# The half block of the first layer follows a table of orders; the product of the small-value gelu becomes a step of its own

## The chip, the cores and the metric

The kernel runs on one core of one Trainium2 chip. The metric is the time of one execution on the device in microseconds (us), the median of several runs. The core's engines each work through a queue of their own in order: TensorE (PE for its matmuls, PEld for its weight loads), VectorE (DVE), ScalarE (ACT), GpSimd (POOL), and SyncE (SP), which only issues DMAs here. They wait for each other through semaphores.

## The reference

```python
# attention with 32 memory rows: batch 8, 8 heads, 576 tokens, head size 64
a = exp(phi - max(phi)); a /= sum(a)                 # over the 32 columns
k_m, v_m = a^T k, a^T v                              # [b, h, 32, 64]
attn = softmax(q k_m^T / 8)                          # [b, h, 576, 32]
x = (attn v_m) with heads side by side               # [4608, 512]
# first layer
h = x @ w_in                                         # [4608, 2048]
x = (h - tanh(h)) @ w_out                            # [4608, 512]
# second layer
h = x @ w_in2
g = where(h > 0, h, exp(min(h, 0)) - 1)
out = g @ w_out2                                     # [4608, 512]
```

The names in the kernel call the function h - tanh(h) of the first layer "g". It is formed in two ways: as a difference where h is large, and as a polynomial product where h is small, since the difference loses digits there. All matmuls of the two layers are done with operands split into a high and a low part, three matmuls for one.

## The kernel before

**Tiling.** The first layer goes through 64 blocks (the loop over `blocks`, L770 to L850). A block is 288 tokens (`n`) by 512 columns of the hidden layer (`sw`), and has two halves (`i`, L809) of 256 hidden columns each. This text counts half blocks from 0 to 127: half 2b is the first half of block b, 2b + 1 its second. The attention units 1 to 15 (generators, `units`), the conversion of the weights from 64-bit words to split 32-bit pairs (generators, `cv`), and the products of the weights with the attention's value rows (`vw_unit`) run between the steps of the half blocks. The second layer follows (L855 to L874).

**A half block.** `h_unit` gives PE 12 matmuls of 288 columns into one of two tiles `h_ps`. On ACT `g_a` forms t = tanh(h), u = h² and s = a square of u; `g_b` forms v = t u on POOL; `g_big` a mask on ACT. On DVE `g_c` forms the difference h - t in place (L394), the product s = (s + G_B) v (L395) and copies the difference over it where the mask is set (L396, `copy_predicated`). The last one frees the `h_ps` tile, which the half after the next one writes. In the next half `g_d` takes the high part of s on ACT (L402) and the low part on POOL (L403). `x_next` gives PE the 12 matmuls of one 128-row piece of x (`x_unit`), of a block about two earlier, into a bank of the pool `ps_m`, and copies them out on ACT (`on_act`, L424) or on DVE (L426). There are two such pieces in a half. `t`, `u`, `v` and the mask have one buffer each, s has two.

**Banks.** The pool `ps_m` has three banks, handed out in turn: to the pieces of x, to the two tiles of a `vw_unit` and to all PSUM tiles of the attention. A tile waits until the bank's former holder has been read.

**Conversions.** One conversion step group costs DVE two instructions (L50 and L51, or L54 and L57) in each half, from block 14 to 57; besides one ACT instruction (L48 or L62), and every second half one on POOL (L64). `cv.round()` moves all conversions by a step, `cv.half()` only those that stand before their first ACT instruction.

**Order.** Nothing reorders: each engine executes in the order in which the program is written (`manual_schedule`), so L811 to L848 set the order on all engines. A `vw_unit` stands ahead of `h_unit` in the second half of each odd block (L811), unless the attention holds it back (`at1.held`); then it comes at L836. `units.round()` is called twice in a half (L832, L846), and lets each live attention unit take one step.

Of the kernel before, what the change touches and what calls it, by code (L numbers as in the profile page):

```python
# [30 lines left out]
G_S = 0.045158483281055074  # L31
G_A = -0.2459677286979875
G_B = 0.27283311065959304


def r32(ap):
# [276 lines left out]
class Moe1:  # L313
# [77 lines left out]
    def g_c(self, n, pg):  # L391
        nc = self.nc
        d, u, t, s, big, v = self.work[n, pg]
        nc.vector.tensor_tensor(d, d, t, op=ALU.subtract)  # L394
        nc.vector.scalar_tensor_tensor(s, s, G_B, v, op0=ALU.add, op1=ALU.mult)  # L395
        nc.vector.copy_predicated(s, big.bitcast(U32), d)  # L396

    def g_d(self, n, pg):
        nc = self.nc
# [143 lines left out]
def moe_kernel(tc, q, k, v, phi, w1, w2, w3, w4, out):  # L543
    nc = tc.nc
    with ExitStack() as top, tc.manual_schedule():
# [157 lines left out]
        def store_late():  # L703
            while late:
                m1.store_x(*late.pop(0))
# [64 lines left out]
        for bi, (ss, bp, sub, j) in enumerate(blocks):  # L770
# [37 lines left out]
            p_there |= p_done  # L808
            for i in range(2):  # L809
                pg = 2 * sw + i  # L810
                if vw_next and bi > 1 and i == 1 and not at1.held:  # L811
                    vw_soon(*vw_next)
                    vw_next = None
                m1.h_unit(sw, n, pg)
                if (bi, i) == (0, 0):
                    cv.round()
                m1.g_a(n, pg)
                m1.g_b(n, pg)
                if i == 1 and bi + 2 < len(blocks):
                    ass, abp, asub, aj = blocks[bi + 2]  # L820
                    far = (2 * ass + asub, 4 * abp + aj)
                    if all(u in p_there for u in range(2 * (far[1] // 2) + 2)):
                        m1.load_p(*far)
                store_late()
                if soon:
                    soon.popleft()()
                x_next(True)
                m1.g_big(n, pg)
                if (bi, i) != (0, 0):
                    cv.round()  # L830
                at1.before_x = True
                units.round()  # L832
                at1.before_x = False
                if pend:
                    m1.g_d(*pend.pop())
                if vw_next and (bi == 1 or i == 1):  # L836
                    vw_soon(*vw_next, i if bi == 1 else None)
                if soon and bi > 60:
                    soon.popleft()()
                x_next(bi < 22)  # L840
                m1.g_c(n, pg)
                cv.half()
                if bi < 7:
                    cv.round()
                    cv.half()
                units.round()  # L846
                pend.append((n, pg))
                next_p(nxt, i == 1)  # L848
            for dm in range(4):
# [55 lines left out]
```

## Time and profile before

| | |
|---|---|
| Median of 3 runs | 1675.61 us (1672.97 to 1678.92) |
| The profiled execution | 1677.41 us, its span 1675.3 us |
| PE busy | 1585.5 us, 95% of the span |
| PEld busy | 1381.5 us, 82% |
| DVE busy | 1201.6 us, 72% |
| ACT busy | 900.9 us, 54% |
| POOL busy | 737.5 us, 44% |

The busy shares are those of the whole span. The first layer's loop ends at about 863 us, and what follows is the second layer, in which PE has almost no gap. A matmul's end is modelled, so that a busy PE can still be waiting between two starts: the pitch from start to start tells how fast it goes. TensorE's granted clock is at its upper level, 2.4 GHz, from about 100 us on, but for a short stretch near 300 us.

### The profile page before, as it was taken

Reading aid. Unit: us, or ns where it says so; the run is one execution under the profiler, and the core shown is the slowest. Engines: PE = TensorE matmul, PEld = TensorE weight load, DVE = VectorE, ACT = ScalarE, POOL = GpSimd, SP = SyncE. Lnnn points to the kernel's source line nnn. Section 1 sums busy time; section 2 is a strip of 40 time slices with the busy share of each in tenths; the row PEclk is TensorE's granted clock in tenths of the full one; section 3 lists DMA queues with packets and bytes.
Section 4 is the critical chain, followed back from the end, with each engine's and each line's share of the span. In section 5 each row is a group of like instructions: output and inputs, shape, how many; then the busy total and the mean of one; then the engine's idle time right before and its main releaser. Section 6 shows DMA issues by size and latency. Waiting matters only on the chain.

```text
span 1675.3 us, 28135 instructions
## 1 busy us (share of the span) xinstructions
PE 1585.5 (95%) x10742; PEld 1381.5 (82%) x10742; DVE 1201.6 (72%) x1680; ACT 900.9 (54%) x1623; POOL 737.5 (44%) x526
## 2 busy tenths in 40 slices
PE   5678989798999999999999999999999999999998
PEld 4557878687999999999999888888888888888886
DVE  5777768878999999999775655656565656555654
ACT  2355768677888888888753333333333333333332
POOL 0245666566775666666642323222232322323222
PEclk9779999999999999999999999999999999999999
DMA  9665667567565456665587321212121212121100
GB/s 238 183 179 159 199 198 238 180 207 240 182 238 170 170 202 214 215 214 189 176 289 279 101 76 38 78 49 76 38 76 46 69 51 63 51 76 51 35 3 26
DMA packets 142214, 232.90 MB, mean 139 GB/s; under 512 B 8704, under 2 KB 102912, under 8 KB 140032
## 3 DMA queue, kind: packets, MB, share of 16 engines
q1 hardware_dynamic: 142080, 231.11, 43.4%
q8 instruction: 84, 1.38, 0.4%
q14 instruction: 50, 0.41, 0.1%
HBM read 157.68 MB, written 73.40 MB: 138 GB/s over the span
## 4 chain that ended last, share of the span: by engine, by line
PE 63%; DVE 9%; issue 2%; POOL 2%; ACT 1%; DMA 0%; DVEq 0%; SPq 0%; POOLq 0%; ACTq 0%
PE h_ps L478 24%; PE o_ps L520 24%; PE x_ps L418 10%; PE h_ps L367 4%; DVE s L395 3%; DVE s L396 2%; DVE h_ps L394 1%; DVE x L426 1%; POOL g L403 1%; POOL v L385 1%; PE vw_ps L349 1%; DVE vw L354 0%; DVE cv_m L50 0%; ACT big L389 0%; DMA p<-p_dram 0%
## 5 line engine op out<-in xcount | busy, mean ns | idle before, releaser
L418 PE MATMUL x_ps<-g,w 128*128 128x288 f32 x3072 | 441.7, 297 | 10.7 <-DVE vw L354 5.4
L504 POOL TENSOR_TENSOR e<-hm,e 128x512 fp32r<-128x512 f32 x144 | 186.7, 1297 | 573.0 <-ACT e L503 529.8
L418 PEld LDWEIGHTS x_ps<-g,w 128*128 128x128 f32 x3072 | 418.0, 189 | 19.0 <-DVE vw L354 9.1
L478 PE MATMUL h_ps<-x,wi 128*128 128x512 f32 (+1 forms) x1920 | 422.2, 370 | 0.0
L520 PE MATMUL o_ps<-wo,e 128*128 128x512 f32 x1728 | 420.3, 392 | 0.7 <-POOL e L504 0.7
L478 PEld LDWEIGHTS h_ps<-x,wi 128*128 128x128 f32 x1920 | 336.0, 188 | 65.7
L520 PEld LDWEIGHTS o_ps<-wo,e 128*128 128x128 f32 x1728 | 323.6, 188 | 72.4 <-POOL e L504 1.1
L489 ACT ACTIVATE t_ps<-hm 128x512 f32<-128x512 f32 x144 | 86.7, 602 | 500.2 <-DVE hm L488 500.2
L385 POOL TENSOR_TENSOR v<-t,u 128x576 f32<-128x576 f32 x128 | 183.5, 1434 | 177.2 <-ACT u L379 129.2
L495 DVE SCALAR_TENSOR_TENSOR hm<-hm,t_ps 128x512 f32<-128x512 f32 x144 | 99.0, 688 | 200.9 <-ACT hm L490 200.9
L367 PE MATMUL h_ps<-p,vw 128*128 128x288 f32 x1536 | 235.5, 303 | 0.0
L403 POOL TENSOR_TENSOR g<-s,g 128x576 fp32r<-128x576 f32 x128 | 192.4, 1503 | 85.8 <-ACT g L402 77.3
L367 PEld LDWEIGHTS h_ps<-p,vw 128*128 128x128 f32 x1536 | 214.1, 192 | 13.7 <-issue 12.4
L395 DVE SCALAR_TENSOR_TENSOR s<-s,v 128x576 f32<-128x576 f32 x128 | 183.7, 1435 | 15.2 <-POOL v L385 15.2
L488 DVE TENSOR_SCALAR hm<-h_ps 128x512 f32<-128x512 f32 x144 | 99.6, 692 | 125.3 <-PE h_ps L478 121.0
L378 ACT ACTIVATE t<-h_ps 128x576 f32<-128x576 f32 x128 | 83.4, 652 | 120.6 <-PE h_ps L367 73.3
L396 DVE COPY_PREDICATED s<-big,h_ps 128x576 f32<-128x576 uint32 x128 | 106.8, 834 | 13.6 <-ACT t L378 0.5
L380 ACT ACTIVATE s<-u,bias 128x576 f32<-128x576 f32 x128 | 99.6, 778 | 20.4 <-POOL g L403 9.8
L394 DVE TENSOR_TENSOR h_ps<-h_ps,t 128x576 f32<-128x576 f32 x128 | 96.9, 757 | 13.4 <-ACT u L379 13.3
L497 DVE TENSOR_TENSOR hm<-hm,h_ps 128x512 f32<-128x512 f32 x144 | 98.9, 687 | 5.0
L496 DVE SCALAR_TENSOR_TENSOR hm<-hm,t_ps 128x512 f32<-128x512 f32 x144 | 98.9, 687 | 5.0
L389 ACT ACTIVATE big<-u,bias 128x576 f32<-128x576 f32 x128 | 98.1, 767 | 0.9 <-DVE s L396 0.2
(88 smaller groups left out, 1559.0 us busy)
## 6 DMA issues: line engine op xcount, KB each, us to landing
x_dram<-x SPq DMA_DIRECT2D x128, 288.0 KB, 2.7
xr<-x_dram SPq DMA_DIRECT2D x72, 512.0 KB, 3.8
p<-p_dram SPq DMA_DIRECT2D x62, 576.0 KB, 5.2
raw<-in_moe_w_in_dram SPq DMA_DIRECT2D x32, 512.0 KB, 4.3
raw<-in_moe_w_out_dram SPq DMA_DIRECT2D x32, 512.0 KB, 4.4
w_dram<-wst SPq DMA_DIRECT2D x32, 512.0 KB, 3.1
kv<-in_k_dram SPq DMA_DIRECT2D x16, 576.0 KB, 6.2
kv<-in_v_dram SPq DMA_DIRECT2D x16, 576.0 KB, 7.7
```

The source lines that it names most:

```text
L367: nc.tensor.matmul(ps[:, j, :NB], lhsT=vw[a][:, kc, c0 + 128 * j:c0 + 128 * j + 128], rhs=p[:, kc, b, :], start=(k == 0), stop=(k == 5))
L380: nc.scalar.activation(s, u, ACTF.Square, bias=bias[:, 0:1], scale=G_S)
L385: nc.gpsimd.tensor_tensor(v, t, u, op=ALU.mult)
L394: nc.vector.tensor_tensor(d, d, t, op=ALU.subtract)
L395: nc.vector.scalar_tensor_tensor(s, s, G_B, v, op0=ALU.add, op1=ALU.mult)
L396: nc.vector.copy_predicated(s, big.bitcast(U32), d)
L403: nc.gpsimd.tensor_tensor(g[:, 1], s, r32(g[:, 0]), op=ALU.subtract)
L418: nc.tensor.matmul(ps, lhsT=wo[pg][a][:, j, 128 * dm:128 * dm + 128], rhs=self.g[n, pg][:, b, j, :], start=(k == 0), stop=(k == 11))
L478: nc.tensor.matmul(out, lhsT=w3[:, a, kc, 128 * j:128 * j + 128], rhs=x[:, b, kc, :], start=(i == 0), stop=(i == 11))
L488: nc.vector.tensor_scalar(hm, w[0], 0.0, None, op0=ALU.min)
L504: nc.gpsimd.tensor_tensor(e[:, 1], hm, r32(e[:, 0]), op=ALU.subtract)
L520: nc.tensor.matmul(acc, lhsT=e[:, a, jj, 128 * tg:128 * tg + 128], rhs=w4[:, b, j, :], start=(k == 0 and jj == 0 and i == 0), stop=(k == l ...
```

## The change

The steps of a half block are written as letters, and a table `PLAN` gives their order: one string for half 0, one for the halves 1 to 13, two strings in turn for the halves 14 to 43 (blocks 7 to 21), two for 44 to 63 (blocks 22 to 31), and four in turn for 64 to 127 (blocks 32 to 63). The first two strings are the order that was there. `g_c` is cut into three steps: d (the difference), e (the product) and p (the predicated copy). X is a piece of x copied on ACT, Y one copied on DVE; U and u are `units.round()`, C is `cv.round()`, c `cv.half()`, G is `g_d`, L the stores of x and a load of p, R the mask, V and W the two places of `vw_unit`, l an entry of `soon`. All engines get the same instructions as before, but for 16 pieces of x whose copy goes from DVE to ACT (84 to 68 copies on DVE). The attention's rounds are called 7 times in a block in blocks 22 to 31, where there were 4.

```diff
+PLAN = ((1, "WHCABLlXRUGVXdepcCcu"),
+        (14, "WHABLlXRCUGVXdepcCcu"),
+        (44, "lWHLABCXRUXGdeVucp", "WcHAlBUXLRCVGdecXup"),
+        (64, "WHAVUBCRlGdULYXUUecp", "WLHuARlCBXVduueYGp"),
+        (128, "WuHALRlBCuVXedGYcpU", "lWHuABXRUdCLuYVuUeGp", "WlHUABYRLCdueXucVGp", "UWHLAVRlCUdXBeXGp"))
...
         nc.vector.tensor_tensor(d, d, t, op=ALU.subtract)
+
+    def g_e(self, n, pg):
...
         nc.vector.scalar_tensor_tensor(s, s, G_B, v, op0=ALU.add, op1=ALU.mult)
-        nc.vector.copy_predicated(s, big.bitcast(U32), d)
+
+    def g_f(self, n, pg):
+        d, u, t, s, big, v = self.work[n, pg]
+        self.nc.vector.copy_predicated(s, big.bitcast(U32), d)
...
-                m1.h_unit(sw, n, pg)
...
-                x_next(bi < 22)
-                m1.g_c(n, pg)
...
+                for step in next(p[(2 * bi + i) % len(p)] for end, *p in PLAN if 2 * bi + i < end):
...
+                    elif step in "XY":
+                        x_next(step == "X")
...
+                    elif step in "Uu":
+                        at1.before_x = step == "U"
+                        units.round()
+                        at1.before_x = False
...
+                    elif step == "V":
+                        if vw_next and (bi == 1 or i == 1):
+                            vw_soon(*vw_next, i if bi == 1 else None)
+                            vw_next = vw_next if bi == 1 and i == 0 else None
...
```

On PE the order changes only in the second halves of blocks 7 to 21, where the attention's matmuls of the first round stand ahead of both pieces of x, and around blocks 22 to 24, where the attention's last rounds come earlier. POOL keeps its order. The places below are on ACT, DVE and PE; after line 32 the changed file's line numbers are higher by 7, and in its loop by 14 or more.

ACT, second half of block 8 (half 17), before. `qT` and `a` belong to the attention: the transposed queries and the exponential of phi, for which the matmuls `km` wait.

```order
L378 ACTIVATE t<-h_ps 128x576
L379 ACTIVATE u<-h_ps 128x576
L380 ACTIVATE s<-u,bias 128x576
L424 ACTIVATE x<-x_ps 128x288
L389 ACTIVATE big<-u,bias 128x576
L201 ACTIVATE qT<-pq 128x288
L166 ACTIVATE a<-a 96x4x6x32
L402 ACTIVATE g<-s 128x576
```

The same place in the changed kernel:

```order
L385 ACTIVATE t<-h_ps 128x576
L386 ACTIVATE u<-h_ps 128x576
L387 ACTIVATE s<-u,bias 128x576
L208 ACTIVATE qT<-pq 128x288
L173 ACTIVATE a<-a 96x4x6x32
L438 ACTIVATE x<-x_ps 128x288
L396 ACTIVATE big<-u,bias 128x576
L416 ACTIVATE g<-s 128x576
```

The exponential moved ahead of a copy of x and of the mask.

DVE, from the first half of block 15 (half 30) into the second, before. `smax`, `rs`, `kvs` and `nmax` are the attention's; `kvs` reads the bank of `km`, which a tile of `vw_unit` takes next.

```order
L395 SCALAR_TENSOR_TENSOR s<-s,v 128x576
L396 COPY_PREDICATED s<-big,h_ps 128x576
L133 TENSOR_REDUCE cmax<-phi 96x128
L50 TENSOR_SCALAR cv_m<-cv_m 128x512
L51 TENSOR_SCALAR cv_m<-cv_m 128x512
L235 TENSOR_REDUCE smax<-s 128x18
L236 TENSOR_SCALAR smax<-smax 128x18
L237 RECIPROCAL smax<-smax 128x18
L183 TENSOR_SCALAR rs<-km 128x1
L184 RECIPROCAL rs<-rs 128x1
L187 TENSOR_SCALAR kvs<-km,rs 128x256
L146 TENSOR_REDUCE nmax<-mT 128x1
```

The same place in the changed kernel:

```order
L406 SCALAR_TENSOR_TENSOR s<-s,v 128x576
L140 TENSOR_REDUCE cmax<-phi 96x128
L410 COPY_PREDICATED s<-big,h_ps 128x576
L242 TENSOR_REDUCE smax<-s 128x18
L243 TENSOR_SCALAR smax<-smax 128x18
L244 RECIPROCAL smax<-smax 128x18
L190 TENSOR_SCALAR rs<-km 128x1
L191 RECIPROCAL rs<-rs 128x1
L194 TENSOR_SCALAR kvs<-km,rs 128x256
L153 TENSOR_REDUCE nmax<-mT 128x1
L57 TENSOR_SCALAR cv_m<-cv_m 128x512
L58 TENSOR_SCALAR cv_m<-cv_m 128x512
```

The two conversion instructions moved behind the attention's, and the predicated copy behind `cmax`.

PE, at the `vw_unit` of block 25 (half 51), with the engines that each row waits for, before:

```order
L349 MATMUL vw_ps<-w_6595,vm 32x256 [waits DVE_49]
L349 MATMUL vw_ps<-w_6595,vm 32x256 [waits Activation_49]
L349 MATMUL vw_ps<-w_6595,vm 32x256 x6
L349 MATMUL vw_ps<-w_6878,vm 32x256 x4
L367 MATMUL h_ps<-p,vw 128x288 [waits PE_49]
```

The same place in the changed kernel:

```order
L356 MATMUL vw_ps<-w_6579,vm 32x256 [waits DVE_49] x2
L356 MATMUL vw_ps<-w_6579,vm 32x256 x6
L356 MATMUL vw_ps<-w_6862,vm 32x256 x4
L374 MATMUL h_ps<-p,vw 128x288 [waits PE_49]
```

The second tile of `vw_ps` takes the bank of the first piece of x in the half before it; that piece was copied on ACT, and is now copied on DVE, behind two conversion instructions and the difference.

DVE, three halves (83 to 85) of blocks 41 and 42, before:

```order
L54 SCALAR_TENSOR_TENSOR cv_m<-raw,cv_m 128x512
L57 SCALAR_TENSOR_TENSOR cv_a<-raw,cv_m 128x512
L426 COPY x<-x_ps 128x288
L394 TENSOR_TENSOR h_ps<-h_ps,t 128x2x288
L395 SCALAR_TENSOR_TENSOR s<-s,v 128x576
L396 COPY_PREDICATED s<-big,h_ps 128x576
L50 TENSOR_SCALAR cv_m<-cv_m 128x512
L51 TENSOR_SCALAR cv_m<-cv_m 128x512
L426 COPY x<-x_ps 128x288
L394 TENSOR_TENSOR h_ps<-h_ps,t 128x2x288
L395 SCALAR_TENSOR_TENSOR s<-s,v 128x576
L396 COPY_PREDICATED s<-big,h_ps 128x576
```

The same place in the changed kernel:

```order
L61 SCALAR_TENSOR_TENSOR cv_m<-raw,cv_m 128x512
L64 SCALAR_TENSOR_TENSOR cv_a<-raw,cv_m 128x512
L406 SCALAR_TENSOR_TENSOR s<-s,v 128x576
L401 TENSOR_TENSOR h_ps<-h_ps,t 128x2x288
L440 COPY x<-x_ps 128x288
L410 COPY_PREDICATED s<-big,h_ps 128x576
L401 TENSOR_TENSOR h_ps<-h_ps,t 128x2x288
L57 TENSOR_SCALAR cv_m<-cv_m 128x512
L58 TENSOR_SCALAR cv_m<-cv_m 128x512
L440 COPY x<-x_ps 128x288
L406 SCALAR_TENSOR_TENSOR s<-s,v 128x576
L410 COPY_PREDICATED s<-big,h_ps 128x576
```

In half 84 the product now stands ahead of the difference and of the copy of x. In half 85 the difference stands ahead of the conversion. Each period of four halves has three copies of x on DVE, where it had four.

## Rows read from the trace of the kernel before

**Rows 1.** Windows: length, then busy us (instructions) of PE, PEld, DVE, ACT, POOL

```profile
198.20:426.10 227.90, 201.27 (x1992) 178.72 (x1991) 183.28 (x269) 166.62 (x334) 143.44 (x101) 0.99 0.68 209
426.10:531.50 105.40, 103.60 (x901) 98.61 (x900) 100.45 (x143) 86.13 (x152) 74.48 (x52) 1.00 0.60 201
...
592.80:802.80 210.00, 206.18 (x1763) 196.82 (x1762) 202.05 (x259) 172.94 (x300) 139.21 (x101) 1.00 0.61 209
...
862.90:1675.30 812.40, 805.95 (x3722) 668.08 (x3721) 466.62 (x647) 281.71 (x476) 229.87 (x163) 1.00 0.23 73
```

**Rows 2.** Waits of PE, 198.2 to 426.1 us: total us, times, longest

```profile
PE km L173 <- ACT a L166: 4.3, 4, 1.4
PE vw_ps L349 <- DVE kvs L187: 4.0, 2, 2.8
PE pq L199 <- ACT x L424: 3.3, 6, 0.8
PE vw_ps L349 <- DVE s L227: 3.3, 3, 1.5
```

**Rows 3.** Timeline in half 17: start us, length us, engine, line, instruction

```profile
224.64 0.39 ACT L424 ACTIVATE x<-x_ps 128x288 f32<-128x288 f32 x1
224.92 0.76 ACT L389 ACTIVATE big<-u,bias 128x576 f32<-128x576 f32 x1
...
225.35 0.76 DVE L395 SCALAR_TENSOR_TENSOR s<-s,v 128x576 f32<-128x576 f32 x1 [0.56 <-POOL v L385]
...
226.77 1.51 PE L173 MATMUL km<-kv,a 96*32 96x192 f32 x32 [1.19 <-ACT a L166]
```

**Rows 4.** Timeline, halves 30 and 31

```profile
330.83 0.68 DVE L50 TENSOR_SCALAR cv_m<-cv_m 128x512 f32<-128x512 f32 x1
...
334.30 1.24 PE L349 MATMUL vw_ps<-w,vm 64*32 64x256 f32 x17 [2.79 <-DVE kvs L187]
```

**Rows 5.** Timeline, halves 42 and 43

```profile
416.13 0.81 DVE L396 COPY_PREDICATED s<-big,h_ps 128x576 f32<-128x576 uint32 x1
...
417.36 1.10 PE L349 MATMUL vw_ps<-w,vm 64*32 64x256 f32 x32 [1.48 <-DVE s L227]
```

**Rows 6.** Timeline, halves 58 and 59

```profile
501.46 0.83 DVE L396 COPY_PREDICATED s<-big,h_ps 128x576 f32<-128x576 uint32 x1
...
503.39 1.09 PE L349 MATMUL vw_ps<-w,vm 64*32 64x256 f32 x32
```

**Rows 7.** Timeline, halves 88 to 91 (cut)

```profile
655.46 3.34 PE L418 MATMUL x_ps<-g,w 128*128 128x288 f32 x24
655.71 0.65 ACT L378 ACTIVATE t<-h_ps 128x576 f32<-128x576 f32 x1 [1.27 <-PE h_ps L367]
...
656.98 1.44 POOL L385 TENSOR_TENSOR v<-t,u 128x576 f32<-128x576 f32 x1 [1.03 <-ACT u L379]
...
658.83 0.46 DVE L426 COPY x<-x_ps 128x288 f32<-128x288 f32 x1
...
659.64 1.42 POOL L403 TENSOR_TENSOR g<-s,g 128x576 fp32r<-128x576 f32 x1
...
659.87 1.81 DVE L395 SCALAR_TENSOR_TENSOR s<-s,v 128x576 f32<-128x576 f32 x1
...
660.46 0.65 ACT L378 ACTIVATE t<-h_ps 128x576 f32<-128x576 f32 x1 [0.62 <-PE h_ps L367]
...
665.22 0.65 ACT L378 ACTIVATE t<-h_ps 128x576 f32<-128x576 f32 x1 [0.63 <-PE h_ps L367]
...
671.23 0.65 ACT L378 ACTIVATE t<-h_ps 128x576 f32<-128x576 f32 x1 [0.57 <-POOL g L403]
```

**Rows 8.** Waits of PE, 592.8 to 802.8 us

```profile
PE x_ps L418 <- DVE vw L354: 3.8, 10, 0.7
```

**Rows 9.** Timeline, half 51

```profile
469.28 0.75 DVE L395 SCALAR_TENSOR_TENSOR s<-s,v 128x576 f32<-128x576 f32 x1
469.31 2.01 POOL L403 TENSOR_TENSOR g<-s,g 128x576 fp32r<-128x576 f32 x1 [1.50 <-ACT g L402]
```

More of the change, by code (lines that the diff above doesn't have):

```diff
@@ L810, in moe_kernel @@
                 pg = 2 * sw + i
-                if vw_next and bi > 1 and i == 1 and not at1.held:
-                    vw_soon(*vw_next)
-                    vw_next = None
-                m1.h_unit(sw, n, pg)
[L815 to L837, printed above, removed]
@@ L838, in moe_kernel @@
-                if soon and bi > 60:
-                    soon.popleft()()
-                x_next(bi < 22)
-                m1.g_c(n, pg)
[L842 to L846, printed above, removed]
+                for step in next(p[(2 * bi + i) % len(p)] for end, *p in PLAN if 2 * bi + i < end):
+                    if step == "W":
+                        if vw_next and bi > 1 and i == 1 and not at1.held:
+                            vw_soon(*vw_next)
+                            vw_next = None
+                    elif step == "H":
+                        m1.h_unit(sw, n, pg)
+                    elif step == "A":
+                        m1.g_a(n, pg)
+                    elif step == "B":
+                        m1.g_b(n, pg)
+                    elif step == "L":
+                        if i == 1 and bi + 2 < len(blocks):
+                            ass, abp, asub, aj = blocks[bi + 2]
+                            far = (2 * ass + asub, 4 * abp + aj)
+                            if all(u in p_there for u in range(2 * (far[1] // 2) + 2)):
+                                m1.load_p(*far)
+                        store_late()
+                    elif step == "l":
+                        if soon:
+                            soon.popleft()()
+                    elif step in "XY":
+                        x_next(step == "X")
+                    elif step == "R":
+                        m1.g_big(n, pg)
+                    elif step == "C":
+                        cv.round()
+                    elif step == "c":
+                        cv.half()
+                    elif step in "Uu":
+                        at1.before_x = step == "U"
+                        units.round()
+                        at1.before_x = False
+                    elif step == "G":
+                        if pend:
+                            m1.g_d(*pend.pop())
+                    elif step == "V":
+                        if vw_next and (bi == 1 or i == 1):
+                            vw_soon(*vw_next, i if bi == 1 else None)
+                            vw_next = vw_next if bi == 1 and i == 0 else None
+                        if soon and bi > 60:
+                            soon.popleft()()
+                    elif step == "d":
+                        m1.g_c(n, pg)
+                    elif step == "e":
+                        m1.g_e(n, pg)
+                    elif step == "p":
+                        m1.g_f(n, pg)
```

2 lines of the change are left out of this document (added).

## The prediction

> **What bounds the kernel now.** I read first where in the span the order can matter, by windows over the stretches that the table names [rows 1]. The second layer with the tail of the first, from 862.9 us on, takes 812.4 us with PE busy for 805.95; the table doesn't reach it, and I give it nothing. What is left are three stretches: halves 14 to 43 (227.9 us), 44 to 63 (105.4 us), and 76 to 115 (210.0 us), the halves in which conversions for the second layer run.
>
> Next I need the time that PE alone would want. A half asks PE for 36 matmuls of 288 columns. In the timeline the starts of tanh follow PE's halves: 655.71 to 660.46 is 4.75 us, and 665.22 to 671.23 is 6.01 us for a half with a `vw_unit` in it [rows 7]. Four halves make 3 x 4.75 + 6.01 = 20.26 us, and PE can't go below. Against that:
> - halves 76 to 115 are ten periods, 202.6 us; they take 210.0, so 7.4 us lie above PE's floor;
> - halves 44 to 63 are five, 101.3 us; they take 105.4, so 4.1 us, the attention's last matmuls among it (I estimate 1 us);
> - halves 14 to 43 are seven and a half, 152 us; they take 227.9. The excess holds the matmuls of some seven attention units, and waits of PE.
>
> The waits of PE in that first stretch name what ends them: the exponential on ACT, `kvs` and the transposes on DVE, copies of x [rows 2]. DVE is busy for 183 of 228 us there [rows 1], so it is not full: PE waits for chains through four engines, not for one engine. In the third stretch DVE is busy for 202.05 of 210.0 us: there DVE is full, and PE's one listed wait, 3.8 us in ten pieces, is for the low parts of `vw` on DVE, which free the bank of the next piece of x [rows 8].
>
> Why DVE is full shows in one half [rows 7]. The product takes 1.81 us from 659.87 on, while POOL works at the low part of g from 659.64 to 661.06. The same product takes 0.76 us where POOL was idle [rows 3]. It meets that POOL instruction because of the order: PE's second piece of x ends at 655.46 + 3.34 = 658.80, its copy on DVE starts at 658.83, then come the difference and the product. Yet v was ready at 656.98 + 1.44 = 658.42.
>
> **First part of the change: blocks 7 to 21.** The same instructions, moved. For each kind of wait in the list [rows 2] I ask whether what ends it moved forward.
> - `km` for the exponential, 4.3 us, four times. In second halves it passes a copy of x and the mask, which reach from 224.64 to 224.92 + 0.76 = 225.68 [rows 3], so 1.0 us of a wait of 1.19. Two of the four stand in second halves; in the other one a conversion's copy is passed too, so its mean wait of 1.1 goes. Together 2.1 us.
> - `vw_ps` for `kvs`, 4.0 us, twice. In the wait of 2.79 us `kvs` passes two conversion instructions, 0.68 us the first [rows 4], so 1.4; in the other the predicated copy, 0.8. Together 2.2.
> - `vw_ps` for the transposes, 3.3 us, three times. They pass the predicated copy, 0.81 us each, with 1.48 us waited in the longest [rows 5]. Together 2.4.
> - `pq` for a copy of x, 3.3 us, six times. In three, the copy passes a copy of g, but PE's next wait, for the transposes, ends where it did before but for the gain above. Nothing more.
>
> The sum is 6.7 us. A wait that closes brings PE sooner to the next one whose end did not move, so I take 5. The lower end is 0 for these edits.
>
> What this part costs: the predicated copy stands behind the attention's instructions on DVE, so that the `h_ps` tile comes free later by up to the 1 or 2 us that they take. The tile is wanted two halves after its own, and a half lasts 227.9 / 30 = 7.6 us here: hidden, by the next half's work. The stores of x move behind a copy on SyncE's queue; the load of p that stands ahead of them is for two blocks on, some 20 us: hidden.
>
> **Second part: blocks 22 to 31.** Here the first piece of x is copied on DVE, behind two conversion instructions and the difference, and the second tile of `vw_unit` wants its bank. By the times of half 58 [rows 6]: the predicated copy ends at 501.46 + 0.83 = 502.29, two conversion instructions take 1.4 us [rows 4], the difference about 0.6 (from 659.29 to 659.87 [rows 7]), the copy 0.46: 504.75. PE reached the `vw_unit` at 503.39. That is 1.4 us late, in five odd blocks: 7.0 us lost. But a wait of PE's gives DVE 1.4 us, and a DVE that is ahead starts the product before POOL's low part of g, and stays ahead. So I take it once or twice, 2 us, against the excess of 3 us without the attention's matmuls, of which I take 2. Net 0; the ends are a loss of 7 and a gain of 3.
>
> **Third part: blocks 32 to 63.** Of four halves, half 0 has its product ahead of the difference and of the copy of x, halves 2 and 3 have no copy of a second piece on DVE, and only half 1 keeps it ahead of the product. So in three of four the product can start when v is ready, at 658.42 in that half, and end 0.76 later, before POOL's next at 659.64. Each that does gives DVE 1.81 - 0.76 = 1.05 us. One copy of x in four, 0.46 us, leaves DVE too. What DVE owes is 7.4 us in ten periods, 0.74 each; one product and the copy cover it, and then PE's floor holds. I take 6 of the 7.4. The ends are 0 and 7.4. The copies go to ACT: ten of about 0.39 us on top of 172.94 in 210 us, so it has room on the whole; if its list in one half grew longer than PE's, tanh of the next half would start late, and that is the lower end of 0.
>
> **The sum.** 5 + 0 + 6 = 11 us. Against the profiled execution, 1677.41 - 11 = 1666.4; that run lies 1.8 us above the median, and against the median it is 1675.61 - 11 = 1664.6, so 1665 us.
>
> **Rivals.** The first: the product only meets another POOL instruction. POOL is busy for 139.21 of 210.0 us in the third stretch [rows 1], so that two of three places meet one. In half 0 the low part of a conversion stands right behind v on POOL, and starts as the product does. Then only the moved copies count, ten of 0.46 us at most, say 4, and the first part's gain is used up by the next wait: 1675.6 - 4 = 1672 us. The Trainium skill, page "SBUF — State Buffer", section "Who interferes with whom", bears on this: a VectorE instruction with two SBUF inputs and a GpSimd one that reads SBUF exclude each other, and whichever issues second stands still until the first is done. The trace agrees both ways: 1.81 us against 0.76, and a low part of g of 2.01 us where the product had started 0.03 us ahead [rows 9]. By that rule the half us or so comes out of POOL instead where the product wins, and where it loses, nothing is gained: this rival's time. For my forecast speaks the 1.2 us in which POOL stands still between v and g [rows 7], against it that every second half has a conversion there.
>
> The second ends slower: banks of `ps_m` come free later than PE wants them. In blocks 22 to 31 that is the 7.0 us worked out above, if DVE doesn't get ahead; in the second halves of blocks 7 to 21 an attention tile now stands right behind `h_unit`, and where it waits as `pq` does on the mean, 3.3 / 6 = 0.55 us [rows 2], eleven of them cost 6.0. With the first part's gain gone and the third part's kept that is 13 - 6 = 7 us slower, 1683 us. It decides from the point where a copy of x ends after PE has come to the bank's next tile; the 1.4 us above says that at today's phase it would.
>
> The third goes further: each attention step on DVE now passes the predicated copy, so that whole chains shorten, and the four lines of the list go altogether, 14.9 us, with 7.4 and 3 from the other parts: 25 us, 1650 us.
>
> **How the numbers follow.** The forecast has 0.50, the first rival 0.22, the slower one 0.15, the larger gain 0.13. A change of over 0.3%, 5.0 us, is about what a measurement of this kernel can tell from none. Faster than 1670.6: nearly all of the forecast (0.48), the larger gain (0.13) and an edge of the first rival (0.03), 0.64. Within 0.3%: the rest of the first rival, of the forecast, and an edge of the slower one, 0.21. Slower: 0.15. The range goes from 1653 to 1677 us; it leaves out most of the slower rival and the far side of the larger gain.
>
> **What the changed kernel's profile would show.** Third part: the ten periods at 203 to 205 us, the wait for the low parts of `vw` gone, the mean product nearer to 0.8 than to 1.8 us in three of four halves. If the products stay at 1.8, the first rival holds. Second part: a wait of `vw_ps` for a copy of x on DVE, once or twice; five times is the slower rival. First part: the waits for the exponential, `kvs` and the transposes shorter by about 1 us each, and 223 us or so for the stretch. What would make the prediction wrong: a chain of the attention that I took for unmoved and that ends later, or ACT turning out full in the halves with two copies of x.

## The result and the profile of the changed kernel

The changed kernel takes 1656.87 us, the median of four runs (1656.48 to 1657.69). Beside them the kernel before took 1677.22 us, also four runs (1672.97 to 1678.92). The ratio is 0.9883, with a 95% interval of 0.9862 to 0.9904: 1.0 to 1.4% faster. Forecast were 1665 us with a range from 1653 to 1677, so the direction held and the time lies in the range, on its lower side. The profiled execution of the changed kernel took 1656.48 us, its span 1654.7 us. One execution of part 2 alone, one of product_between and two of copies_only took 1968 to 4639 us, and the medians of these three kernels below leave them out.

The same stretches as in [rows 1], cut again at the starts of tanh, by windows over the changed kernel. The columns are the stretch, its length, the busy time and number of instructions of PE, PEld, DVE, ACT and POOL, the granted TensorE clock, and the DMA's share and rate. In this order the rows are halves 14 to 43, 44 to 63, 76 to 115, and all from half 116 on:

```profile
195.20:413.60 218.40, 199.18 (x1992) 177.51 (x1990) 182.04 (x269) 167.05 (x333) 143.93 (x101) 0.99 0.72 216
413.60:518.50 104.90, 103.46 (x898) 98.62 (x899) 96.38 (x145) 86.52 (x152) 74.17 (x52) 1.00 0.61 200
579.40:782.80 203.40, 203.40 (x1762) 196.39 (x1761) 173.12 (x248) 175.12 (x309) 144.52 (x101) 1.00 0.68 215
782.80:1654.70 871.90, 865.31 (x4216) 726.07 (x4214) 505.30 (x697) 328.20 (x555) 269.96 (x189) 1.00 0.25 83
```

Against [rows 1] the first stretch is shorter by 9.5 us, the second by 0.5, the third by 6.6. In the third PE is now busy in all of 203.40 us, and DVE fell from 202.05 to 173.12 us although it lost only ten of its copies. Halves 64 to 75 (61.3 to 60.9 us) and the rest of the program (872.5 to 871.9) give another 1.0. The remaining 3.0 us of the difference between the two spans lie ahead of half 14 (198.2 to 195.2 us), where the order is the same in both; the section on the hardware comes back to them.

The waits of PE in halves 14 to 43 of the changed kernel, the lines that answer to [rows 2]: the waiting tile, who ended the wait, us in all, times, longest.

```profile
PE bmax L160 <- POOL dmax L157: 6.1, 3, 3.4
PE km L180 <- ACT a L173: 2.1, 3, 1.4
PE vw_ps L356 <- DVE kvs L194: 2.0, 2, 1.6
PE pq L206 <- ACT x L438: 1.7, 3, 0.7
PE vw_ps L356 <- DVE s L234: 1.7, 3, 0.9
PE x_ps L432 <- DVE kvs L194: 1.1, 2, 0.6
PE km L180 <- ACT x L438: 1.1, 2, 0.6
PE mT L151 <- ACT x L438: 0.3, 1, 0.3
```

The four lines on which the first part's sum was built fell from 14.9 us [rows 2] to 7.5. Two lines of 1.1 us each are new: x_ps for kvs, and km for a copy of x on ACT, which reads the bank that km wants.

Next the timeline of four halves of the third stretch, 88 to 91, the places of [rows 7]; first DVE, then POOL (start, duration, engine, line, operation). L406 is the product (L395 before), L417 the low part of g, L71 the low part of a conversion:

```profile
643.16 1.84 DVE L406 SCALAR_TENSOR_TENSOR s<-s,v 128x576 f32<-128x576 f32 x1 [1.72 <-ACT big L396]
649.38 0.75 DVE L406 SCALAR_TENSOR_TENSOR s<-s,v 128x576 f32<-128x576 f32 x1
653.84 0.84 DVE L406 SCALAR_TENSOR_TENSOR s<-s,v 128x576 f32<-128x576 f32 x1
658.69 0.76 DVE L406 SCALAR_TENSOR_TENSOR s<-s,v 128x576 f32<-128x576 f32 x1
...
643.08 1.30 POOL L71 TENSOR_TENSOR wst<-cv_a,wst 128x512 fp32r<-128x512 f32 x1
644.34 1.95 POOL L417 TENSOR_TENSOR g<-s,g 128x576 fp32r<-128x576 f32 x1
649.99 1.43 POOL L417 TENSOR_TENSOR g<-s,g 128x576 fp32r<-128x576 f32 x1 [1.50 <-ACT g L416]
654.72 1.44 POOL L417 TENSOR_TENSOR g<-s,g 128x576 fp32r<-128x576 f32 x1 [0.65 <-ACT g L416]
660.44 1.43 POOL L417 TENSOR_TENSOR g<-s,g 128x576 fp32r<-128x576 f32 x1 [1.78 <-DVE s L410]
```

Three of four products are short: each starts 0.6 to 1.8 us ahead of POOL's low part of g. The fourth, in half 88, starts 0.08 us behind the conversion's instruction on POOL and takes 1.84 us; PE loses nothing by it, and DVE had stood idle for 1.72 us ahead of it. Over the stretch, in the list of groups by line (the count, then busy us and mean ns of one, then the idle time ahead of them):

```profile
L406 DVE SCALAR_TENSOR_TENSOR s<-s,v 128x576 f32<-128x576 f32 x40 | 41.6, 1040 | 18.2 <-ACT big L396 18.2
```

### The profile page after: what moved, and what is told of

Its sections match the earlier page's. It is cut to its first block, busy times and chain, and to the rows that moved or that the text cites. A ratio compares the mean times of both kernels' runs of the same rounds, so it can differ in the third digit from the quotient of the medians.

```text
span 1654.7 us, 28097 instructions
## 1 busy us (share of the span) xinstructions
PE 1580.8 (96%) x10742; PEld 1380.2 (83%) x10742; DVE 1143.8 (69%) x1664; ACT 906.7 (55%) x1639; POOL 744.6 (45%) x526
## 4 chain that ended last, share of the span: by engine, by line
PE 81%; DVE 6%; ACT 4%; issue 4%; POOL 3%; DMA 1%; SPq 0%; POOLq 0%; ACTq 0%; DVEq 0%
PE h_ps L492 24%; PE o_ps L534 24%; PE x_ps L432 19%; PE h_ps L374 10%; PE vw_ps L356 2%; PE km L180 1%; DVE s L406 1%; POOL v L392 1%; DMA q<-in_q_dram 1%; POOL g L417 1%; ACT t L385 1%; ACT u L386 1%; DMA raw<-in_moe_w_in_dram 1%; DVE h_ps L401 0%; ACT x L438 0%
## 5 line engine op out<-in xcount | busy, mean ns | idle before, releaser
L417 POOL TENSOR_TENSOR g<-s,g 128x576 fp32r<-128x576 f32 x128 | 198.2, 1549 | 115.4 <-ACT g L416 91.5
L374 PEld LDWEIGHTS h_ps<-p,vw 128*128 128x128 f32 x1536 | 214.4, 192 | 13.2 <-issue 11.7
L406 DVE SCALAR_TENSOR_TENSOR s<-s,v 128x576 f32<-128x576 f32 x128 | 137.2, 1072 | 54.3 <-ACT big L396 35.7
L401 DVE TENSOR_TENSOR h_ps<-h_ps,t 128x576 f32<-128x576 f32 x128 | 97.1, 759 | 18.9 <-ACT u L386 18.5
L504 ACT ACTIVATE hm<-hm 128x512 f32<-128x512 f32 x144 | 91.0, 632 | 13.1
```

What stands on the lines that cost most here:

```text
L374: nc.tensor.matmul(ps[:, j, :NB], lhsT=vw[a][:, kc, c0 + 128 * j:c0 + 128 * j + 128], rhs=p[:, kc, b, :], start=(k == 0), stop=(k == 5))
L417: nc.gpsimd.tensor_tensor(g[:, 1], s, r32(g[:, 0]), op=ALU.subtract)
```

## The experiments

All of them are written as tables of orders for the changed kernel's loop. "The old order" is the string `WHABLlXRCUGVXdepcu` in halves 14 to 43 and `WHABLlXRCUGVYdepcu` from half 44 on.

### The three parts one by one

```
part1_alone:  (44, new, new), (64, old), (128, old)
part2_alone:  (44, old), (64, new, new), (128, old)
part3_alone:  (44, old), (64, old), (128, new, new, new, new)
```

> Only halves 14 to 43 follow their new strings; from half 44 on the old order stands in the table. Theory: the three parts act each in their own stretch, so halves 14 to 43 take the 218.4 us of the changed kernel (227.9 before), the rest what it took before, and the time is 9.5 us below before, near 1667.5 us. Rival: part of the 9.5 us is only there because of what follows (the halves from 44 on take the work in sooner); then the stretch ends at 222 us or later. On the 3.0 us which halves 0 to 13 were shorter by, though their order did not change: if they differ from run to run, half 14 starts anywhere between 195 and 198.5 us here; if the program's new form made them, at 195.2.

> Only halves 44 to 63 follow their new strings. Theory: 104.9 us in place of 105.4 for these halves, 0.5 us in all, which is not measurable. Rival: without the new order ahead of it DVE arrives later in its work at half 44, and the bank of the second tile of vw_unit is late in each odd block: up to 1.4 us in each of five, 112 us for the stretch and 7 us slower. Halves 0 to 13 as in the kernel with the first part alone.

> Only halves 64 to 127 follow their new strings. Theory: halves 76 to 115 take 203.4 us as in the changed kernel (210.0 before), with a mean product of about 0.9 us in place of 1.65, and the time is 6.6 to 7 us below before, near 1670.5 us. Rival: the gain needs the DVE that the second part leaves ahead; then the products meet POOL's low part of g as before, 1.5 us or more each, and halves 76 to 115 take 208 to 210 us.

Measured against the kernel before in the same session (1676.13 us): part 1 alone 1665.99 us, ratio 0.9939 (0.9926 to 0.9953); part 2 alone 1675.20 us, 0.9995 (0.9983 to 1.0007); part 3 alone 1668.14 us, 0.9946 (0.9931 to 0.9961). The three ratios multiplied give 0.9880, and the whole change gave 0.9883. Windows over the one stretch that each changes (part 2 alone has 104.90 us for its own, as the changed kernel has), first part 1 alone:

```profile
195.10:413.70 218.60, 199.25 (x1992) 177.75 (x1991) 182.18 (x269) 167.12 (x333) 144.02 (x101) 0.99 0.72 215
```

and part 3 alone:

```profile
590.90:794.40 203.50, 203.50 (x1762) 196.49 (x1761) 173.07 (x248) 175.29 (x310) 144.80 (x101) 1.00 0.68 215
```

Each is within 0.2 us of the changed kernel's stretch, and for the three stretches the three theories held. (The expectation that halves 0 to 13 take as long in part 2 alone as in part 1 alone did not: half 14 starts at 199.6 us in the one and at 195.1 in the other; the section on the hardware tells why.) So the parts act each in its own place and add up, and none needs what another leaves behind. In the second part the rival with the late banks did not come: in that stretch the changed kernel's PE waits once for a copy of x on ACT, 0.9 us, and for none on DVE. The products there became shorter instead, from 1393 ns on the mean to 1095.

### What in the third part gives the gain

Two kernels take one element of it each into the old order, in halves 64 to 127. In the first the product stands ahead of the second copy of x and ahead of the difference; in the second every fourth half copies its second piece on ACT.

```
product_ahead:  - "WHABLlXRCUGVYdepcu"   + "WHABLlXRCUGVeYdpcu"
copies_only:    - "WHABLlXRCUGVYdepcu"   + the same in three of four halves, "WHABLlXRCUGVXdepcu" in the fourth
```

> The old order but for one step: in halves 64 to 127 the product stands ahead of the second copy of x and of the difference; all copies stay on DVE. Theory (the product's place gives the gain, since it then ends before POOL's low part of g starts): products of 0.75 to 0.9 us in halves 76 to 115, and 203 to 204 us for them in place of 210.0, 6 to 7 us in all. Rival (the copies that went to ACT give the gain): the products meet POOL's next instruction all the same, 1.5 us or more, and the stretch stays at 208 to 210 us. A third way: the product now waits for v and holds the copy of x behind it; then PE waits for x's copy and the stretch takes over 210 us.

> The old order but for one thing: in every fourth half from 64 on the second piece of x is copied on ACT in place of DVE, 16 copies in all, ten of them in halves 76 to 115. Theory: DVE gains 0.46 us in each, but the products of the three other halves still stand behind a copy that waits for PE's second piece, and so still meet POOL's low part of g (1.6 to 1.85 us); in the fourth half the product moves forward by 0.46 us and may pass. Halves 76 to 115: 4 to 5 us less without that, 206 us, and PE's floor, 203 us, if the fourth product drops to 0.75 us as well, since 0.46 + 0.7 us is more than the 0.74 us that DVE owes in a period. Rival (the product's place is needed): 208 us or more.

The kernel product_ahead took 1679.53 us, ratio 1.0020 (1.0007 to 1.0032): the third of the ways expected, but for another reason than the one written down. PE's only listed wait in halves 76 to 115 is for vw on DVE, 3.1 us in ten, as before the change. The stretch takes 212.6 us, and DVE is not full in it (188.19 us):

```profile
591.30:803.90 212.60, 209.50 (x1762) 198.28 (x1761) 188.19 (x259) 170.70 (x300) 149.27 (x101) 1.00 0.61 207
```

The timeline of its half 88 shows what holds; ACT, POOL and DVE follow one another, and the last row is ACT's tanh of half 89:

```profile
654.99 0.65 ACT L385 ACTIVATE t<-h_ps 128x576 f32<-128x576 f32 x1 [1.02 <-DVE h_ps L401]
...
656.26 1.44 POOL L392 TENSOR_TENSOR v<-t,u 128x576 f32<-128x576 f32 x1 [0.79 <-ACT u L386]
657.66 1.30 POOL L71 TENSOR_TENSOR wst<-cv_a,wst 128x512 fp32r<-128x512 f32 x1
...
657.74 1.84 DVE L406 SCALAR_TENSOR_TENSOR s<-s,v 128x576 f32<-128x576 f32 x1 [0.60 <-POOL v L392]
659.50 0.45 DVE L440 COPY x<-x_ps 128x288 f32<-128x288 f32 x1
659.87 0.75 DVE L401 TENSOR_TENSOR h_ps<-h_ps,t 128x576 f32<-128x576 f32 x1
...
660.73 0.65 ACT L385 ACTIVATE t<-h_ps 128x576 f32<-128x576 f32 x1 [1.62 <-DVE h_ps L401]
```

The tile t has one buffer, and the difference is its last reader. With the difference behind the product, a closed chain arises: tanh, u, v, product, copy of x, difference, and the next half's tanh waits 1.62 us for that. Its length from tanh to tanh is 5.74 us where the product meets the conversion's instruction on POOL, as here, and 4.65 us in the next half, where the product takes 0.76 us: 10.39 us for two halves in which PE wants 9.50. The two others of the period take 5.71 and 5.16 us; together that is 21.26 us against 20.26, and ten periods give the 212.6. So this kernel could not decide between the two theories: it had moved two things. In the next one difference and product keep their order, and the copy of x moves behind both.

```
product_between:  - "WHABLlXRCUGVYdepcu"   + "WHABLlXRCUGVdeYpcu"
```

> The old order but for one step: in halves 64 to 127 the product stands ahead of the second copy of x, but behind the difference, so that tanh of the next half is not held up as it was with the product ahead of both. Theory (the copy of x ties the product to the end of PE's second piece, and so to POOL's low part of g): products of 0.75 to 0.85 us in the halves without a conversion on POOL, 1.84 us at most in the others, and halves 76 to 115 at 203 to 205 us in place of 210.0. Rival (the copies on ACT are needed as well): the stretch stays at 207 us or more. If halves 0 and 2 of a period each meet the conversion's instruction on POOL, DVE's sum for a period is about 20.2 us, as long as PE's, and the stretch may lie at 204 to 206 us.

It took 1670.05 us, ratio 0.9965 (0.9953 to 0.9977). Its third stretch, and the group of the product in it:

```profile
591.50:795.00 203.50, 203.50 (x1762) 196.49 (x1761) 184.78 (x258) 171.84 (x300) 149.38 (x101) 1.00 0.63 216
```

```profile
L406 DVE SCALAR_TENSOR_TENSOR s<-s,v 128x576 f32<-128x576 f32 x40 | 51.7, 1292 | 15.7 <-POOL v L392 15.7
```

That one swap reaches the 203.5 us of the whole third part, with all copies left on DVE. Its products take 1.84 and 1.83 us in halves 0 and 2 of a period, behind the conversion's instruction, and 0.75 us in halves 1 and 3; two short ones of four are enough, and DVE stands idle for 15.7 us ahead of products. (The difference moved ahead of the copy as well; that the product's length is what counts is shown by g_low_zero below, in which neither moves.)

The kernel copies_only took 1674.95 us, ratio 0.9993 (0.9984 to 1.0003), and its stretch 209.7 us: not the 206 us or less of the theory, but the rival's 208 or more. The ten copies did leave DVE, but the mean product rose from 1673 to 1741 ns:

```profile
L406 DVE SCALAR_TENSOR_TENSOR s<-s,v 128x576 f32<-128x576 f32 x40 | 69.6, 1741 | 0.0
```

In the half without the copy on DVE (half 91) the product starts sooner, and into the very same instruction on POOL; first POOL, then DVE:

```profile
674.61 1.42 POOL L417 TENSOR_TENSOR g<-s,g 128x576 fp32r<-128x576 f32 x1 [1.50 <-ACT g L416]
...
674.75 1.90 DVE L406 SCALAR_TENSOR_TENSOR s<-s,v 128x576 f32<-128x576 f32 x1
```

It takes 1.90 us where the products of this half in a period took 1.42 us on the mean in the kernel before. Of the 4.7 us that DVE was spared in copies (18.3 to 13.6), 2.7 went into products (40 times 0.068 us). The copies are no part of the gain.

The last question on this part is whether POOL's low part of g is what makes the product long at all. Here the old order stands throughout, and that instruction is replaced:

```
- nc.gpsimd.tensor_tensor(g[:, 1], s, r32(g[:, 0]), op=ALU.subtract)
+ nc.gpsimd.memset(g[:, 1].bitcast(F32), 0.0)        # halves 64 to 116
```

> The old order throughout. In halves 64 to 116 the low part of g is set to zero on POOL in place of the subtraction, so that POOL reads neither s nor g for it (this part of the result is left out there). Nothing moves on DVE, PE or ACT. Theory (the product is long because it runs beside POOL's low part of g): products of 0.75 us in the halves without a conversion's instruction on POOL, and about the same in the others, where that instruction stands right behind v and is over before the product, which comes behind the copy of x, starts; halves 76 to 115 take 203 to 204 us in place of 210. Rival (the product is long for another reason, such as DMA traffic or ACT's reads beside it): 1.4 us or more as before, and 208 to 210 us.

It took 1670.11 us, ratio 0.9954 (0.9938 to 0.9971), with 203.5 us for the stretch. The product and the memset in it:

```profile
L406 DVE SCALAR_TENSOR_TENSOR s<-s,v 128x576 f32<-128x576 f32 x41 | 30.7, 749 | 0.0
L418 POOL MEMSET g<- 128x576 f32 x40 | 23.3, 582 | 0.0
```

All forty products are short in the unchanged place, behind the copy of x. The theory holds in both directions: move the product away from the instruction, or take the instruction away from the product, and the stretch comes to PE's floor. (The memset also runs earlier than the subtraction did, right behind v or the conversion, and is shorter, so that it hardly meets the product; this kernel doesn't say what a memset beside a product would cost.)

### What in the first part gives the gain

Two steps were moved alone, in halves 14 to 43 of the old order.

```
U_ahead:  - "WHABLlXRCUGVXdepcu"   + second halves "WHABLlUXRCGVXdepcu"
p_last:   - "WHABLlXRCUGVXdepcu"   + all halves "WHABLlXRCUGVXdecup"
```

> The old order but for one step: in the second halves of blocks 7 to 21 the attention's first round stands ahead of the first piece of x, of the mask and of the conversion step. If this step is the main part of the first stretch's gain (the exponential, the transposes and kvs each pass a copy, the mask and two conversion instructions), halves 14 to 43 take 220 to 222 us in place of 227.9 and the waits of PE for the exponential and for kvs fall by a half. If the gain comes from the predicated copy's place or from the copy of x ahead of that of g, the stretch stays at 226 to 228 us. From half 44 on all as before.

> The old order but for one step: in halves 14 to 43 the predicated copy stands behind the attention's second round. By the prediction's terms it gives 0.8 us at each of three waits for the transposes and at one for kvs, so 2 to 3 us: 225 us for halves 14 to 43 in place of 227.9. If the attention's first round was the main part, no more than 3 us here; if the predicated copy was, 221 us or less.

U_ahead took 1671.65 us, ratio 0.9974 (0.9963 to 0.9984), and 221.8 us in the stretch; p_last 1672.67 us, 0.9980 (0.9970 to 0.9991), and 222.9 us. In seven kernels with the old order in these halves the stretch took 226.2 to 229.5 us, 227.6 on the mean, so that the two steps give 5.8 and 4.7 us. By the medians they give less, 3.9 and 2.9 us: the profiled execution of U_ahead, 1665.17 us, is the fastest of its ten, that of p_last, 1668.76 us, the second fastest. What went, by the waits of PE in the stretch of U_ahead:

```profile
PE vw_ps L356 <- DVE s L234: 3.2, 3, 1.5
PE pq L206 <- ACT x L438: 2.6, 5, 0.8
PE km L180 <- ACT a L173: 1.8, 3, 0.8
PE vw_ps L356 <- DVE kvs L194: 1.2, 1, 1.2
PE mT L151 <- ACT x L438: 0.3, 1, 0.3
```

and of p_last:

```profile
PE vw_ps L356 <- DVE kvs L194: 2.9, 2, 2.6
...
PE vw_ps L356 <- DVE s L234: 0.6, 1, 0.6
```

Against [rows 2] the round ahead of x takes 2.5 us from the wait for the exponential, 2.8 from kvs (of which 1.4 come back as x_ps waiting for kvs), 0.7 from pq, and most of 1.8 us in which the matmul mT had waited for a copy of x; the transposes (3.2) it leaves as they were. The predicated copy's place takes 2.7 of the 3.3 us at the transposes and 1.1 at kvs, and leaves the rest (pq 3.3 and mT 1.6 us). The expectation of p_last, 2 to 3 us, was too low by the stretch, though not by the median; that of U_ahead held in its stretch. Both together, with the changed kernel's order from half 44 on:

```
U_and_p:  - "WHABLlXRCUGVXdepcu"   + "WHABLlXRCUGVXdecup" and "WHABLlUXRCGVXdecup" in turn
```

> In halves 14 to 43 two steps alone are moved from the old order: the attention's first round ahead of the first piece of x in second halves, and the predicated copy behind the attention's second round in all halves. From half 44 on the order is that of the changed kernel. Alone, the two gave 6.1 and 5.0 us in this stretch. Theory: they close the same kind of waits, and what is left of them are the waits for dmax on POOL, so that together they give about what the whole strings gave: 217 to 219 us for halves 14 to 43, and a time near that of the changed kernel, 1655 to 1659 us. Rival: the other moves of the strings (the conversion steps, the copy of x ahead of that of g) carry a part: 221 us or more, and 1660 us.

220.1 us for the stretch, 7.8 of the 9.5, and 1659.95 us in all, ratio 0.9895 (0.9872 to 0.9918). That lies between what theory and rival expected. The two steps are the greater part; whether the conversion steps and the copy of x ahead of that of g give the last 1.7 us stays open, since the stretch scatters by as much among kernels with the same order in it.

### The same orders in blocks 1 to 6

```
new_strings_from_2:  (2, old), (14, "lWHLABCXRUXGdeVucCcp", "WcHAlBUXLRCVGdecCcXup"), then as changed
U_and_p_from_2:      (2, old), (14, "WHABLlXRCUGVXdecCcup", "WHABLlUXRCGVXdecCcup"), then as changed
```

> The changed kernel with its two strings for blocks 7 to 21 used from half 2 on (the additional conversion steps of blocks 1 to 6 kept, behind the attention's first round). In halves 2 to 13 PE waits for the exponential, for kvs, for the transposes and for vw. Theory: these chains pass the predicated copy and the conversions as they do in the later stretch; halves 2 to 13, 111 to 114 us in the kernels so far, take 3 to 6 us less, and the time is 1651 to 1654 us. Rival: these waits are for loads and for the one attention unit in flight, or the conversions arrive later and vw_unit's weights with them: no gain, or some us lost. A product or transposed maximum that meets POOL in halves 5 to 7 adds 3 to 4 us to either by chance.

> The changed kernel, but in halves 2 to 13 two steps are moved: the attention's first round ahead of the first piece of x in second halves, the predicated copy behind everything in all halves; the conversion steps stay where they were. Theory: half of what the full strings would give there, 2 to 3 us less than the changed kernel, since fewer chains are shortened but no conversion is delayed. Rival: no change, 1656 to 1658 us, because the waits of these halves end with loads.

new_strings_from_2 took 1658.45 us (ratio 0.9895, 0.9875 to 0.9916), U_and_p_from_2 1656.08 us (0.9883, 0.9858 to 0.9907). Halves 2 to 13 took 113.1 and 112.0 us, no less than the 110.8 of the changed kernel. In both, PE waits for vw on DVE grew (x_ps for vw, 1.0 us in the changed kernel, 3.1 and 2.2 here), and the longest ones stayed: 3.2 us for converted weights, 2.8 for the queries, and 4.1 for the transposes, which ends ahead of tanh of half 2 and so before the stretch begins. The theories, 3 to 6 and 2 to 3 us less, did not come. Half 7 alone takes 13.2 to 17.9 us among kernels with one order, as the section on the hardware shows. Without it the eleven other halves take 95.5 and 97.3 us here, and 95.2 to 97.6 us in the twelve kernels that have the old order in them. So no gain is shown, as the rivals had it; which of these waits could be moved stays open. Neither version can be told from the changed kernel in time, and none beats it.

## Why the prediction was right, and where it was off

**The floor and the stretches.** Right. PE's floor of 20.26 us for four halves holds: ten periods take 203.40 us against 202.6, and all that follows half 115, the second layer in it, moved by no more than 0.6 us of 872.5.

**First part, forecast 5 us, measured 9.5.** The mechanism was right, the term was mis-sized. Idle time of PE, the stretch less PE's busy time, went from 227.90 - 201.27 = 26.6 us to 218.40 - 199.18 = 19.2, so 7.4 us are waits; the full lists of waits add up to the same, 26.3 us before and 18.9 after. They divide the 7.4 so:

- The three terms of the sum, 6.7 us forecast, gave 5.8: the exponential 2.2 (forecast 2.1), kvs 2.0 (2.2), the transposes 1.6 (2.4).
- Waits that the sum had at nothing gave 5.9: pq for a copy of x 1.6, the matmul mT for one 1.5, the second tile of `vw_unit` for one 1.0, smaller ones 1.8. "Nothing more" was the wrong step here. The line of mT before the change, which [rows 2] leaves out:

```profile
PE mT L144 <- ACT x L424: 1.8, 2, 1.6
```

- New or longer waits took back 4.3: x_ps for kvs 1.1, km for a copy of x 1.1, smaller ones 2.1. I had cut 6.7 to 5 for such a loss, so it was more than twice what I allowed. The line of km shows how it comes: of the two waits for the exponential in second halves, 1.19 and 1.23 us, 0.59 and 0.51 are left, now for the bank.

So that 5 and 7.4 lie so near each other is in part luck: 5.9 us not counted stood against 2.6 us of loss too few and 0.9 of the terms too many. The rest is PE's busy time, which fell by 2.1 us with the same matmuls. Half 31 shows 1.25 us of that; most of the rest lies in halves 28 and 29, and what gives it is not shown. In the kernel before the granted clock behind the wait of 2.79 us [rows 4] was:

```profile
334.00:336.00 2.00, 1.70 (x32) 1.06 (x32) 0.32 (x2) 0.04 (x1) 2.00 (x3) 0.63 1.03 363
336.00:338.00 2.00, 2.00 (x15) 1.82 (x9) 1.09 (x2) 1.09 (x2) 0.59 (x2) 0.52 0.09 37
```

and in the changed kernel, where the same wait lasts 1.60 us:

```profile
326.00:328.00 2.00, 1.92 (x38) 1.54 (x39) 1.45 (x4) 0.79 (x3) 0.42 (x1) 1.00 1.00 285
```

After the longer wait the engine ran near its lower level, 1.2 GHz, for some 3 us; after the shorter one it stayed at 2.4 GHz. PE's busy time in half 31 went from 8.09 to 6.84 us. A wait that long costs more than its own length here, and the sum had no term for that. The other drop of the clock, in half 28, behind the wait for dmax (3.0 us before, 3.4 after), is in both kernels. (In the kernel before the clock also falls for a few us near 114 and near 149 us: the words "but for a short stretch near 300 us" ahead of the prediction leave these out.)

**Second part, forecast 0, measured 0.5 in the stretch and nothing that can be told from zero in time.** The zero was right, its two terms were not. The banks cost nothing, where I had put 2 us: DVE gets ahead, as I argued, the products there are shorter by 0.3 us, and PE never waits for a copy of x on DVE. And the gain of 2 us was hardly there to be had: PE stood idle for only 105.40 - 103.60 = 1.8 us of the stretch before the change [rows 1], and for 1.4 after it. Of the 4.1 us above the floor I had taken 1 for the attention's matmuls; PE's busy time makes it 103.60 - 101.3 = 2.3.

**Third part, forecast 6 us, measured 6.6.** Right in size and in cause, and three of four products are short, as counted. Three steps of it were wrong. Which half loses: I had taken it to be half 1, where the copy stays ahead of the product; it is half 0, whose product stands behind v and so beside the conversion's instruction, the point that the first rival had raised. It lost only its own 1 us, since half 1 and the others make DVE early enough. And the gain of the moved copies: I counted 0.46 us in each period towards what DVE owed; copies_only shows that they give nothing by themselves, and product_between that nothing of them is needed. And a reading: in the half of [rows 7], half 88, POOL does not stand still for the 1.2 us between v (to 658.42) and the low part of g (from 659.64). The rows had left out what fills them:

```profile
658.38 1.29 POOL L64 TENSOR_TENSOR wst<-cv_a,wst 128x512 fp32r<-128x512 f32 x1
```

The pause that I built on is real only in the halves without a conversion on POOL, 1.40 us in half 89 and 1.50 in half 91.

The rule that the prediction took from the Trainium skill ("SBUF — State Buffer", "Who interferes with whom") holds in these rows: whichever of the two issues second stands still. Where the product is first, POOL's low part of g takes 1.95 us in place of 1.43; where POOL is first, the product takes 1.8 in place of 0.75.

**The rivals.** The first (the product only meets another instruction on POOL) fell with the changed kernel's products and with product_between: the product does meet one in half 0, and that has no price, since the short ones of the other halves are enough. The slower one fell with the second stretch; its other half, attention tiles that hold up second halves, shows as the 1.1 us of km waiting for a copy of x, in halves 17 and 37, in place of the 6.0 us in eleven. The larger gain came half way: its four lines went from 14.9 to 7.5 us, not to none.

**The sum.** 9.5 + 0.5 + 6.6 + 1.0 = 17.6 us by the stretches of the two profiled executions, against 11 forecast; the medians differ by 20.4 us in one session, and the three parts alone by 10.1 + 0.9 + 8.0 = 19.0. Of the 20.4 us, 3.0 lie ahead of half 14 in the profiled executions, where the order did not change, and are not shown to be the change's.

## What to carry to other kernels

If an instruction of one engine has two quite different durations in a trace, look for the instruction of the other engine beside it: here moving the copy of x behind the difference and the product gave the stretch the same 203.5 us as rewriting four strings, while taking work off the full engine gave nothing. When moving an instruction earlier, list what it is moved past that frees a single-buffered tile: the product past the copy of x gained, the product past the difference as well lost it again. Price a long wait of TensorE with the clock that follows it, not by its length alone: in the traces here one of 1.60 us had no such price, one of 2.79 us had 1.25 us of it.

## What the runs showed of the hardware

**A product can stand still behind two instructions in a row.** Halves 0 to 13 have the same order in nearly all of these kernels, and yet half 7 takes 17.7 us in the kernel before and 17.9 in U_and_p, but 13.2 us in the changed kernel and in U_ahead. The cause stands in half 6. In the kernel before, first DVE, then POOL, then the matmul of half 7 that waits:

```profile
139.20 3.39 DVE L395 SCALAR_TENSOR_TENSOR s<-s,v 128x576 f32<-128x576 f32 x1
...
138.76 1.83 POOL L161 TENSOR_TENSOR a<-phi,bm 96x768 f32<-96x768 f32 x1 [0.39 <-ACT bm L159]
140.54 1.42 POOL L403 TENSOR_TENSOR g<-s,g 128x576 fp32r<-128x576 f32 x1
...
146.61 0.61 PE L199 MATMUL pq<-ident,q 96*128 96x96 f32 x3 [2.55 <-DVE vw L354]
```

and in the changed kernel:

```profile
139.00 1.35 DVE L406 SCALAR_TENSOR_TENSOR s<-s,v 128x576 f32<-128x576 f32 x1
```

The product of 3.39 us issued in the middle of one instruction on POOL and did not get in before the next one either: it ended 0.63 us behind the second. DVE comes to vw 3.4 us behind the tanh of half 7 (145.93 to 142.56), in the changed kernel 0.1 us behind it; PE waits 2.55 us for vw, and soon after the granted clock falls to 0.63 for 3 us:

```profile
148.00:151.00 3.00, 3.00 (x19) 3.00 (x19) 3.00 (x5) 1.49 (x3) 3.00 (x3) 0.63 0.91 248
```

Where the product has one instruction of POOL to wait for and not two, all of it is gone, 4.5 us in half 7. The twelve kernels with the same order there divide cleanly: in eight the product takes 3.38 to 3.40 us and half 7 16.2 to 17.9, in four 1.17 to 1.35 us and 13.2. In the profiled executions the start of half 14 lies anywhere from 192.4 to 199.6 us among kernels whose order up to there is the same. So the 3.0 us ahead of half 14 are not shown to come from the change; that the four runs of the changed kernel lie within 1.2 us, and those of the kernel before within 6, may be this too, but only the profiled execution of each can be looked into.

**The long product restores itself.** In the kernel with the second part alone the last seven products ahead of half 64 take 0.76 us each; with half 64 the old order begins, and the first product there takes 1.56 us. The last product of half 63, then POOL's low part of g and the product of half 64:

```profile
528.72 0.76 DVE L406 SCALAR_TENSOR_TENSOR s<-s,v 128x576 f32<-128x576 f32 x1 [0.63 <-ACT big L396]
...
534.40 1.43 POOL L417 TENSOR_TENSOR g<-s,g 128x576 fp32r<-128x576 f32 x1 [0.97 <-ACT g L416]
534.89 1.56 DVE L406 SCALAR_TENSOR_TENSOR s<-s,v 128x576 f32<-128x576 f32 x1
```

A lead of DVE is lost at once: the copy of x, which now stands ahead of the product, waits 1.95 us for PE's piece and starts at 533.86, the difference follows, and by then POOL has begun the low part of g.
